# Attention with decay and a SwiGLU FFN in one kernel: K and Q transposed by DMA, decay moved into V

## Chip, cores, metric

The kernel runs on one core of a Trainium2 chip. The metric is device time in microseconds (us) of one launch. The profile is one execution taken by the hardware profiler. TensorE is PE in it (PEld its weight loads), VectorE DVE, ScalarE ACT, GpSimd POOL, SyncE SP.

## The reference

Eight batches, eight heads, 576 tokens, 64 elements per head; then an FFN over 4608 tokens of width 512, inner width 1536.

```python
scores = scale * np.matmul(q, k.transpose(0, 1, 3, 2))
cum = np.cumsum(np.maximum(s, 0.0), axis=-1)
bias = -(cum[:, :, :, None] - cum[:, :, None, :])
scores = np.where(causal, -1000000000.0, scores + np.minimum(bias, 0.0))
attn = softmax(scores)                    # max subtracted, sum + 1e-9
x = np.matmul(attn, v)                    # heads side by side: 4608 x 512
xn = x / np.sqrt(np.mean(x * x, -1) + 1e-6) * rms_g
g = xn @ w_gate
out = (g * sigmoid(g) * (xn @ w_val)) @ w_out
```

The part of the bias that depends on the query cancels in the softmax. What is left is a factor exp(cum) of the key.

## The kernel before

**Two streams of work.** The FFN runs in 9 chunks of 512 tokens (`ffn`). A chunk has 12 blocks of 128 inner columns, each with four gate matmuls (line 632, "G") and four value matmuls (641, "V"), and then four output blocks of 12 matmuls (654, "O"). ACT makes a tanh of the gate (635); DVE makes U (644) and Ht (637) of it.

Attention is cut into small steps that are put between the FFN's groups. After each group the program calls `step`, one slot: 36 slots in a chunk. `step` looks at queues written by hand (`s_seq`, `av_seq`, `xt_seq`, `t_seq` and the side queues) and issues what is ready, by lags counted in slots (`can_s`, `can_av`, `can_t`). All this is settled when the program is built. On the chip each engine goes through its own list in order and waits on semaphores.

**One attention batch.** A batch has five token blocks (four of 128, one of 64).

- K and Q come from memory as float32 on the SP queue (batches 0 and 1) or the ACT queue, four tokens (1 KB) in a piece (`load_kq`), the last 64 tokens apart (`load_kq_tail`). POOL, ACT or DVE cast them to bf16 (`cast`, `cast_x`, lines 138, 140, 148).
- For batches 0 and 1, and for K throughout, TensorE transposes (`t_step`, 173; `tail_step`, 189) and ACT or DVE copies out of PSUM. Q of later batches is transposed by a DMA on SP (`kq_dma`, 160).
- `s_step` (236): the scores of one key block against its own and the next query block, for four heads: four matmuls of 256 columns into one double bank of PSUM (`psS`, one buffer). One exponential per head follows on ACT (260), because its bias is a column per head: `biasK` holds the cumulated decay, less half of its range. POOL masks the diagonal block (269).
- `av_step` (286, 292): values for one query block and four heads; the 65th column of V is 1, so that it yields the sum. DVE divides (299, 301).
- The norm: sum of squares on ACT (307), two small operations on POOL (314, 317), scaling on DVE (324), a transposing DMA to `xnT` on SP (334), or TensorE in batch 0 (343).

V is loaded and cast by POOL's DMA queue (`load_v`, 164), as are the FFN weights (`load_w`, two halves each, 666). A range check of K and Q runs on DVE (`check_mag` 355, `check_max` 361). If it fails, a second, slow path (`general`) computes all again; it does not run with these inputs.

**The start.** The first four token blocks of batch 0 are done before the FFN's first chunk, in an order written out by hand, with some filling matmuls (`warm`).

Of the kernel before, what the change touches and what calls it, by code (L numbers as in the profile page):

```python
# [26 lines left out]
def kernel(  # L27
# [22 lines left out]
    HP = H // 2  # L50
    NV = 65
# [19 lines left out]
    pp = fast.enter_context(tc.tile_pool(name="pp", bufs=1, space=bass.MemoryType.PSUM))  # L71


    xnT = mp.tile([128, CC, RING], BF16, name="xnT")

    kq32 = mp.tile([128, 2, H, 320], FP32, name="kq32")
    kqn = mp.tile([128, 2, 2, NSC, H, D], BF16, name="kqn")
    kqT = mp.tile([128, 2, 2, HP * 640], BF16, name="kqT")


    kqTn = kqT.rearrange("d a w (h n) -> d a w h n", h=HP)
    kqTx = kqT.rearrange("d a w (c h n) -> d a w c h n", c=NSC, h=HP)
    XB = 2
    v_sb = mp.tile([128, 2, NSC, H, NV], BF16, name="v_sb")

# [5 lines left out]
    biasK = mp.tile([128, NSC, BH], FP32, name="biasK")  # L91
# [3 lines left out]
    mag = mp.tile([128, H * 320], BF16, name="mag")  # L95
# [3 lines left out]

    def psF():  # L100
        return pp.tile([128, DM], FP32, name="psF", tag="F", bufs=4)

    def psF16():
        return pp.tile([128, 8, 128], BF16, name="psF16", tag="F", bufs=4)

    def psS():
        return pp.tile([128, 2, 512], FP32, name="psS", tag="S", bufs=1)

    def psAV():
        return pp.tile([128, 512], FP32, name="psAV", tag="AV", bufs=1)  # L110

    def psAV16():
        return pp.tile([128, 8, 128], BF16, name="psAV16", tag="AV", bufs=1)

    def psT():
        return pp.tile([128, 8, 128], BF16, name="psT", tag="T", bufs=1)

    def psT32():
        return pp.tile([128, 512], FP32, name="psT32", tag="T", bufs=1)


    def load_kq(eng, b, w, h0=0, h1=H):
        src = k if w == 0 else q
        eng.dma_start(
            out=kq32[:, w, h0:h1, 0:256],
            in_=src[b, h0:h1, 0:512, :].rearrange("h (p r) d -> p h (r d)", r=4))

    def load_kq_tail(eng, b, w):
        src = k if w == 0 else q
        eng.dma_start(  # L130
            out=kq32[0:64, w, :, 256:320],
            in_=src[b, :, 512:576, :].rearrange("h p d -> p h d"))

    def cast(eng, b, w, r0, r1, h0=0, h1=H):
        o = kqn[:, b % 2, w, r0:r1, h0:h1, :]
        i = kq32[:, w].rearrange("p h (r d) -> p r h d", d=D)[:, r0:r1, h0:h1, :]
        if eng is nc.scalar:
            eng.activation(out=o, in_=i, func=AF.Copy)  # L138
        else:
            eng.tensor_copy(out=o, in_=i)  # L140

    def cast_x(eng, b, w, hp):

        if hp < HP:
            o = kqn[:, b % 2, w, 0:4].rearrange("p r h d -> p (r h d)")[:, hp * 512:hp * 512 + 512]
            o = o.rearrange("p (r h d) -> p h r d", r=4, h=2)
            i = kq32[:, w, 2 * hp:2 * hp + 2, 0:256].rearrange("p h (r d) -> p h r d", d=D)
            eng.tensor_copy(out=o, in_=i)
        else:
            cast(eng, b, w, 4, 5)  # L150

    def kq_dma(b, w, c):

        if c < 4:
            src = kqn[32 * c:32 * c + 32, b % 2, w, 0:4].rearrange("p r h d -> p (r h d)")
            dst = kqTx[:, b % 2, w, c].rearrange("d h (r p) -> d (h r) p", r=4)
        else:
            src = kqn[0:64, b % 2, w, 4].rearrange("p h d -> p (h d)")
            dst = kqTx[:, b % 2, w, 4, :, 0:64]
        nc.sync.dma_start_transpose(out=dst, in_=src)  # L160

    def load_v(b, c):
        n = rows(c)
        nc.gpsimd.dma_start(  # L164
            out=v_sb[0:n, b % 2, c, :, 0:64],
            in_=v[b, :, c * 128:c * 128 + n, :].rearrange("h p d -> p h d"))


    def t_step(b, hp, w, pT=None, dve=None):
        pT = psT() if pT is None else pT  # L170
        dve = (w == 1) if dve is None else dve
        for r in range(4):
            nc.tensor.matmul(  # L173
                pT[:, r, :], lhsT=kqn[:, b % 2, w, r, 2 * hp:2 * hp + 2, :],
                rhs=ident_bf, is_transpose=True, start=(r == 0), stop=(r == 3))
        dst = kqTn[:, b % 2, w, hp, 0:512].rearrange("d (p r) -> d p r", r=4)
        src = pT[:, 0:4, :].rearrange("d r p -> d p r")
        if dve:
            nc.vector.tensor_copy(out=dst, in_=src)
        else:  # L180
            nc.scalar.activation(out=dst, in_=src, func=AF.Copy)

    def tail_step(b):
        pT = psT()
        nw = 2 if b < XB else 1
        for w in range(nw):
            for hp in range(HP):
# [5 lines left out]
        if b == 0:  # L193
            nc.vector.tensor_copy(out=dst, in_=src)
        else:
            nc.scalar.activation(out=dst, in_=src, func=AF.Copy)
# [14 lines left out]
    def slot_free():  # L211
        return eread.get(ecount[0] % NE, 0) == 0
# [850 lines left out]
```

## Time and profile before

| | |
|---|---|
| median of 3 runs | 384.63 us (384.48 to 384.88) |
| profiled execution, first to last instruction | 383.2 us |
| granted TensorE clock, mean | 0.995 |
| TensorE busy | 349.6 us (91%) |
| VectorE, ScalarE, GpSimd busy | 286.1, 247.4, 172.7 us |
| exponentials (line 260) | 352, 114.3 us busy |
| first FFN matmul | at 32.36 us |
| DMA | 46.24 MB, 103292 packets, of them 78481 under 512 B |

The time around the span is not in the profile; the runs are 1.3 to 1.7 us above it. Busy times of engines overlap. Matmuls are pipelined, so the distance between the starts of two groups tells more than the duration in a row.

### The profile page before, as it was taken

Reading aid. Unit: us, or ns where it says so; the run is one execution under the profiler, and the core shown is the slowest. Engines: PE = TensorE matmul, PEld = TensorE weight load, DVE = VectorE, ACT = ScalarE, POOL = GpSimd, SP = SyncE. Lnnn points to the kernel's source line nnn. Section 1 sums busy time; section 2 is a strip of 40 time slices with the busy share of each in tenths; the row PEclk is TensorE's granted clock in tenths of the full one; section 3 lists DMA queues with packets and bytes.
Section 4 is the critical chain, followed back from the end, with each engine's and each line's share of the span. In section 5 each row is a group of like instructions: output and inputs, shape, how many; then the busy total and the mean of one; then the engine's idle time right before and its main releaser. Section 6 shows DMA issues by size and latency. Waiting matters only on the chain. (4 is left out here: it accounts for less than half of the span.)

```text
span 383.2 us, 7015 instructions
## 1 busy us (share of the span) xinstructions
PE 349.6 (91%) x2391; PEld 165.5 (43%) x2436; DVE 286.1 (75%) x525; ACT 247.4 (65%) x646; POOL 172.7 (45%) x277
## 2 busy tenths in 40 slices
PE   1767999899999999999989999999999999999992
PEld 1443544444444444444434444444444444444441
DVE  6768988499888879987988977984388539837720
ACT  3777787457886687768678757776986774323311
POOL 5866725956774496619734764362223220000000
PEclk9999999999999999999999999999999999999997
DMA  7999999999998896796559083981200221020011
GB/s 232 183 229 232 141 221 179 149 200 196 131 187 214 172 173 98 197 201 51 78 186 225 16 89 92 122 63 42 98 15 9 55 98 21 3 83 28 2 56 60
DMA packets 103292, 46.24 MB, mean 121 GB/s; under 512 B 78481, under 2 KB 98449, under 8 KB 103249
## 3 DMA queue, kind: packets, MB, share of 16 engines
q0 software_dynamic: 41168, 9.44, 30.5%
q1 hardware_dynamic: 43184, 21.97, 26.6%
q10 hardware_dynamic: 18896, 14.30, 15.3%
q8 instruction: 21, 0.34, 0.4%
q14 instruction: 23, 0.18, 0.2%
HBM read 38.16 MB, written 9.44 MB: 124 GB/s over the span
## 5 line engine op out<-in xcount | busy, mean ns | idle before, releaser
L260 ACT ACTIVATE E<-psS,biasK 128x256 bf16<-128x256 f32 (+3 forms) x352 | 114.3, 427 | 8.7 <-PE psS L236 7.6
L641 PE MATMUL psF<-xnT,wv_sb 128*128 128x512 bf16 x417 | 110.0, 380 | 1.0 <-DVE Ht L637 0.2
L632 PE MATMUL psF<-xnT,wg_sb 128*128 128x512 bf16 x419 | 109.1, 379 | 1.8 <-ACT xnT L350 0.7
L654 PE MATMUL psF<-wout_sb,Ht 128*128 128x512 bf16 x416 | 100.8, 379 | 0.8 <-issue 0.2
L269 POOL TENSOR_SCALAR_AFFINE_SELECT E<-E 128x512 bf16<-128x512 bf16 x72 | 52.8, 733 | 94.8 <-ACT E L260 94.1
L635 ACT ACTIVATE T<-psF 128x512 f32<-128x512 f32 x108 | 64.5, 600 | 46.8 <-PE psF L632 40.1
L644 DVE SCALAR_TENSOR_TENSOR U<-T,psF 128x512 bf16<-128x512 f32 x108 | 73.7, 682 | 22.3 <-ACT T L635 22.1
L637 DVE TENSOR_TENSOR Ht<-U,psF 128x512 bf16<-128x512 bf16 x99 | 67.6, 683 | 7.1 <-PE psS L236 0.5
L632 PEld LDWEIGHTS <-wg_sb 128*128 128x128 bf16 x432 | 38.9, 97 | 42.8 <-issue 4.8
L654 PEld LDWEIGHTS <-Ht 128*128 128x128 bf16 x432 | 38.6, 98 | 42.8 <-issue 3.3
L641 PEld LDWEIGHTS <-wv_sb 128*128 128x128 bf16 x432 | 38.1, 98 | 43.0 <-issue 6.4
L324 DVE SCALAR_TENSOR_TENSOR xs_sb<-x_sb,al_all,g_row 128x512 bf16<-128x512 bf16 (+1 forms) x40 | 33.6, 842 | 16.0 <-POOL al_all L317 15.2
L307 ACT ACTIVATE xs_sb<-x_sb 128x512 bf16<-128x512 bf16 (+1 forms) x36 | 22.8, 637 | 32.5 <-DVE x_sb L301 31.8
L659 ACT ACTIVATE osb<-psF 128x512 f32<-128x512 f32 x36 | 21.7, 602 | 28.2 <-PE psF L654 20.2
L164 POOL DMA_DIRECT2D v_sb<-in_v_dram x40 | 35.4, 884 | 0.0
L140 POOL CAST kqn<-kq 128x512 bf16<-128x512 f32 (+1 forms) x46 | 32.6, 728 | 3.9 <-DMA kq<-in_k_dram 3.9
L361 DVE TENSOR_TENSOR acc<-acc,mag 128x1280 bf16<-128x1280 bf16 x32 | 32.4, 1034 | 0.3
L314 POOL TENSOR_SCALAR al_all<-ss_all 128x1 f32<-128x1 f32 (+1 forms) x40 | 10.9, 272 | 45.2 <-ACT xs_sb L307 40.2
L236 PE MATMUL psS<-kqT 64*128 64x256 bf16 (+2 forms) x304 | 26.6, 261 | 3.7 <-ACT E L260 2.5
L292 PEld LDWEIGHTS <-E 128*128 128x128 bf16 x320 | 22.3, 99 | 13.9 <-POOL E L269 3.5
L173 PE MATMUL psT<-ident_bf,kqn 128*128 128x128 bf16 x124 | 13.9, 227 | 12.2 <-ACT kqn L138 8.3
L317 POOL TENSOR_TENSOR al_all<-al_all,mhalf 128x1 f32<-128x1 f32 (+1 forms) x40 | 23.2, 581 | 3.3
(93 smaller groups left out, 288.3 us busy)
## 6 DMA issues: line engine op xcount, KB each, us to landing
out_dram<-osb SPq DMA_DIRECT2D x36, 256.0 KB, 2.2
kq<-in_q_dram ACTq DMA_DIRECT2D x6, 1024.0 KB, 8.5
kq<-in_k_dram ACTq DMA_DIRECT2D x6, 1024.0 KB, 7.7
v_sb<-in_v_dram POOLq DMA_DIRECT2D x32, 128.0 KB, 4.6
wg_sb<-in_moe_w_gate_dram POOLq DMA_DIRECT2D x2, 768.0 KB, 7.3
wv_sb<-in_moe_w_val_dram POOLq DMA_DIRECT2D x2, 768.0 KB, 10.4
wout_sb<-in_moe_w_out_dram POOLq DMA_DIRECT2D x1, 1536.0 KB, 14.4
kq<-in_k_dram SPq DMA_DIRECT2D x2, 512.0 KB, 6.5
```

The lines of the kernel that those rows point to most:

```text
L140: eng.tensor_copy(out=o, in_=i)
L164: nc.gpsimd.dma_start(out=v_sb[0:n, b % 2, c, :, 0:64], in_=v[b, :, c * 128:c * 128 + n, :].rearrange("h p d -> p h d"))
L260: nc.scalar.activation(out=eo, in_=ei, func=AF.Exp, scale=0.125, bias=biasK[:, kb, bh:bh + 1])
L269: nc.gpsimd.affine_select(out=Ev[:, :, 0:nq], in_=Ev[:, :, 0:nq], pattern=[[0, nh], [1, nq]], compare_op=ALU.is_ge, fill=0.0, base=0, chan ...
L324: nc.vector.scalar_tensor_tensor(out=xs_sb[0:n, (b * NSC + qb) % NX, :], in0=x_sb[0:n, (b * NSC + qb) % NX, :], scalar=al_all[0:n, col:col ...
L361: nc.vector.tensor_tensor(out=acc[:, sl], in0=acc[:, sl], in1=mag[:, sl], op=ALU.max)
L632: nc.tensor.matmul(Gp, lhsT=wg_sb[:, cc, fs], rhs=xnT[:, cc, x0:x0 + DM], start=(cc == 0), stop=(cc == CC - 1))
L635: nc.scalar.activation(out=T, in_=Gp, func=AF.Tanh, scale=0.5)
L637: nc.vector.tensor_tensor(out=Ht[:, fb - 1, :], in0=pend[0], in1=pend[1], op=ALU.mult)
L641: nc.tensor.matmul(Vp, lhsT=wv_sb[:, cc, fs], rhs=xnT[:, cc, x0:x0 + DM], start=(cc == 0), stop=(cc == CC - 1))
L644: nc.vector.scalar_tensor_tensor(out=U, in0=T, scalar=1.0, in1=Gp, op0=ALU.add, op1=ALU.mult)
L654: nc.tensor.matmul(Op, lhsT=Ht[:, fb, tb * 128:(tb + 1) * 128], rhs=wout_sb[:, fb, :], start=(fb == 0), stop=(fb == FB - 1))
```

## The change

- K and Q are loaded by token blocks, one block of one tensor for all heads at a time, cast by the DMA on POOL's queue (pieces of 64 float32). One transposing DMA on SP turns a block of K and Q together. TensorE transposes only in batch 0.
- Decay: `wK` = exp(cum less half of its range) for each key and head is made once. V is loaded as float32 on SP and multiplied by `wK` (`weigh_v`: POOL, in batch 0 DVE). The column of ones becomes `wK` itself (`weigh_one`).
- With no bias left, an exponential covers four heads. `s_step` issues the matmuls of all eight heads in one run, into two buffers of a PSUM tile `psW`, which `av_step` shares. `av_step` does eight heads in one tile, with one reciprocal and one division.
- The sum of squares is always on ACT (`x_sum`). The range check reads the transposed K and Q.
- Weights come in thirds. Values may follow scores after 4 slots (before 5). The hand-written order of the start is new, and the lags are others; attention steps end in chunk 5 of the built order (before: chunk 7).

The core of the diff:

```diff
+    def load_kq(b, c, w):
+        n = rows(c)
+        nc.gpsimd.dma_start(
+            out=kq[0:n, b % 2, c, w].rearrange("p (h d) -> p h d", d=D),
+            in_=(k if w == 0 else q)[b, :, c * 128:c * 128 + n, :].rearrange("h p d -> p h d"))
+
+    def kq_dma(b, c):
+        n = rows(c)
+        nc.sync.dma_start_transpose(
+            out=kqT[:, b % 2, c].rearrange("d w h n -> d (w h) n")[:, :, 0:n],
+            in_=kq[0:n, b % 2, c].rearrange("p w e -> p (w e)"))
...
+        nc.sync.dma_start(
+            out=v32[0:n, b % 2, c],
...
+    def weigh_v(eng, b, c):
+        n = rows(c)
+        eng.tensor_tensor(
+            out=v_sb[0:n, b % 2, c, :, 0:D], in0=v32[0:n, b % 2, c],
+            in1=wK[0:n, c, b * H:(b + 1) * H].unsqueeze(2).to_broadcast([n, H, D]), op=ALU.mult)
+
+    def weigh_one(eng, b):
+        eng.tensor_copy(out=v_sb[:, b % 2, :, :, D], in_=wK[:, :, b * H:(b + 1) * H])
...
-                    nc.scalar.activation(out=eo, in_=ei, func=AF.Exp, scale=0.125,
-                                         bias=biasK[:, kb, bh:bh + 1])
...
+        for g in ((0,) if kb == 4 else (0, 1)):
+            e = take_slot((b, kb, g), 1 if kb == 4 else 2)
+            ps = psW()
+            hps = range(HP) if kb == 4 else (2 * g, 2 * g + 1)
+            for j, hp in enumerate(hps):
+                for par in (0, 1):
...
+                    nc.tensor.matmul(
+                        ps[:, par, j * W:(j + 1) * W], lhsT=kqT[rs, p, kb, 0, hp, :], rhs=qT,
+                        start=(j == 0), stop=(j == len(hps) - 1))
...
+            def exps(eo=eo, ei=ei):
+                nc.scalar.activation(out=eo, in_=ei, func=AF.Exp, scale=0.125)
...
+            if c == NSC - 1:
+                check(b)
+            if b + 2 < B:
+                t = slot[0]
+                loads(b + 2, lambda: slot[0] >= t + 6 and slot[0] % 2 and phase() < 30)
...
+        return ready(4, "S", b, qb) and (b == 0 or ready(3, "V", b, qb))
...
-        fs = slice(i * (DF // 2), (i + 1) * (DF // 2))
+        fs = slice(i * (DF // 3), (i + 1) * (DF // 3))
...
+    def decay_exp(ps):
+        nc.scalar.activation(out=wK.rearrange("p a e -> p (a e)"), in_=ps[:, 0:NSC * BH], func=AF.Exp)
...
+        load_kq(0, 0, 0)
+        load_kq(0, 0, 1)
+        make_identity(nc, ident_bf)
+        load_kq(0, 1, 1)
+        load_kq(0, 1, 0)
...
+        t_step(0, 0, True)
+        t_step(0, 1, True)
+        t_step(1, 1, True)
+        s0 = scores(0)
+        s0[0][0]()
+        s0[1][0]()
+        ps = decay_turn()
...
+        check(0)
+        loads(1, lambda: True)
+        dma_side.insert(6, (lambda: True, lambda: load_w(moe_w_gate, wg_sb, 2)))
+        dma_side.insert(7, (lambda: True, lambda: load_w(moe_w_val, wv_sb, 2)))
+        dma_side.append((lambda: True, lambda: nc.gpsimd.dma_start(
+            out=wout_sb, in_=moe_w_out.rearrange("(fc p) d -> p fc d", p=128))))
+        values(1, lambda: slot[0] >= 8)
+        weighs(1)
```

In `step`, a slot now takes from the SP queue either a transposing DMA or a V load, and from POOL's two queues (`dma_side`, `pool_side`) one entry; a mask of the step before goes ahead of them.

## The prediction

> **What bounds the kernel now.** I read the page's busy times first, then the windows, then TensorE's timeline.
>
> ```profile
> span 383.2 us, 7015 instructions
> PE 349.6 (91%) x2391; PEld 165.5 (43%) x2436; DVE 286.1 (75%) x525; ACT 247.4 (65%) x646; POOL 172.7 (45%) x277
> ```
>
> A matmul's end is modelled, so 91% alone proves little. The windows (PE, PEld, DVE, ACT, POOL busy in each stretch) say more:
>
> ```profile
> 184.00:222.00 38.00, 36.23 (x272) 16.90 (x276) 32.99 (x60) 30.73 (x85) 21.29 (x34) 1.00 0.61 127
> 345.00:376.50 31.50, 31.18 (x142) 14.03 (x145) 17.51 (x31) 9.32 (x18) 0.00 (x0) 1.00 0.09 35
> ```
>
> The second row is a chunk of FFN alone: 31.2 us for 144 matmuls, 0.216 us each. The first is about a chunk with attention mixed in: it lasts some 39 us. So TensorE's order sets the time, and attention costs what it puts into that order. TensorE's timeline prices each piece by the distance of starts:
>
> ```profile
> 45.12 1.03 PE L632 MATMUL psF<-xnT,wg_sb 128*128 128x512 bf16 x4
> 46.08 0.39 PE L236 MATMUL psS<-kqT 64*128 64x256 bf16 x4
> 46.41 0.40 PE L173 MATMUL psT<-ident_bf,kqn 128*128 128x128 bf16 x4
> 46.64 1.03 PE L641 MATMUL psF<-xnT,wv_sb 128*128 128x512 bf16 x4
> 47.50 0.39 PE L173 MATMUL psF<-ident_bf,kqn 128*128 128x128 bf16 x4
> ```
>
> Four FFN matmuls take 0.86 us (46.64 to 47.50), but 0.96 ahead of scores (45.12 to 46.08): entering scores costs 0.10. Four score matmuls take 0.33 less rounding, 0.32; a transposing step of four 0.22, 0.055 each. Values are 0.0305 each (eight in 0.24 to 0.25 elsewhere in this timeline); eight 64-column scores take 0.22 plus the 0.10.
>
> The sum for before, from the first FFN matmul at 32.36 to the last one's end near 376.4: FFN 1296 x 0.216 = 279.9; scores 56 x 0.42 + 8 x 0.32 = 26.1; values 520 x 0.0305 = 15.9; K and Q transposes (128 + 36) x 0.055 = 9.0; x transposes 8 x 0.055 = 0.4. Total 331.3. The stretch is 344.0, so 12.7 us are stalls: on single-buffered score PSUM, on K copies in chunk 0, on the last x tile of chunk 0 (1.5 us). Around it lie 32.4 us of start and 383.2 - 376.4 = 6.8 us of end. The runs' median, 384.63, is 1.4 us above this span; I add that at the end.
>
> **Part 1, transposes leave TensorE.** The built order of the changed kernel has no K or Q transpose after the start: -9.0 us on the path. Batches 1 to 7 need 35 transposing DMAs instead, twice the size of today's 30.
>
> **Part 2, eight score matmuls in one run.** 28 runs replace 56 steps of 256 columns: 28 x (0.64 + 0.10) = 20.7 against 23.5, -2.8 us. The built order does show eight in a row, so that rival is out. Values keep their 520 matmuls.
>
> So TensorE's own work is 279.9 + 20.7 + 2.6 + 15.9 + 0.4 = 319.5 us.
>
> **Part 3, one exponential per four heads.** These are the rows (line, engine, operation, shapes, count, busy us, mean ns):
>
> ```profile
> L260 ACT ACTIVATE E<-psS,biasK 128x256 bf16<-128x256 f32 x180 | 71.9, 484 | 4.5 <-PE psS L236 3.4 <-DVE biasK L684 0.5 <-issue 0.2
> L659 ACT ACTIVATE osb<-psF 128x512 f32<-128x512 f32 x36 | 21.7, 602 | 28.2 <-PE psF L654 20.2 <-remote 5.0 <-PEq L892 2.0
> L140 POOL CAST kqn<-kq 128x512 bf16<-128x512 f32 x42 | 29.8, 727 | 0.1
> L164 POOL DMA_DIRECT2D v_sb<-in_v_dram x40 | 35.4, 884 | 0.0
> L269 POOL TENSOR_SCALAR_AFFINE_SELECT E<-E 128x512 bf16<-128x512 bf16 x72 | 52.8, 733 | 94.8 <-ACT E L260 94.1
> ```
>
> ACT took 415 ns for 256 elements (the first casts) and 602 for 512, 0.73 ns per element; 1024 come to 0.97 us. 64 of these and 8 of 0.6 make 67 us against 114.3 on ACT. The K copies (some 23 us) go as well. ACT was not the bound, so this shortens only the chain from scores to values.
>
> That chain gets less room. Values now come 4 slots after their scores, formerly 5. By the built order, score run, four FFN groups, values: 0.75 + 4 x 0.866 = 4.2 us from the first score to the first value, 4.45 to the second half. In between: 0.45 to the first half's scores, 0.97 exponential, a tanh (0.6) that must await its FFN group and so ends at 2.2, the second exponential to 3.2, its mask on POOL 0.73: 3.95. The margin is 0.5 us, when nothing is ahead of the mask on POOL. I put 0.15 us of wait on each of 36 value steps, 5 us (bounds 0 and one POOL issue of 0.88 each).
>
> **Part 4, POOL.** Per batch it now has 10 K/Q loads x 0.88, five weighings, one copy of the ones column (0.3), 9 masks x 0.73 and 5 pairs for the norm at 0.85: the weighing has no row. It reads two tensors where the cast reads one: between 0.73 and twice that; I take 1.1, midway. 8.8 + 5.0 + 0.3 + 6.6 + 4.3 = 25.0 us, with bounds 23.3 and 26.6, in the 33.8 us that TensorE gives a batch ((319.5 + 11 - 3 x 31.2) / 7: attention now ends in chunk 5, and three chunks are FFN alone). So POOL is 74% full, with masks queued behind loads. The Trainium skill (GPSIMD Engine Reference, section 3.1) puts a two-input elementwise operation on that engine at about 2.6 cycles per element at 1.2 GHz, by which 512 elements would be an estimated 1.1 us. No run here shows it; it would leave POOL at 25.0.
>
> **Part 5, DMA.** K and Q come in pieces of 256 B (today 1 KB), through POOL's queue like V today; V moves to SP. Three windows of 1 us in which the DMA engines were full (at 41, 206 and 201 us) price packets:
>
> ```profile
> q0 software_dynamic: 1207, 0.16, 240.6%
> q10 hardware_dynamic: 364, 0.37, 105.2%
> q1 hardware_dynamic: 916, 0.26, 129.8%
> ```
>
> The first is V alone, 1207 pieces of 256 B read, 0.31 MB per us; the second K/Q alone in 1 KB, 0.37 MB; the third mostly transposes. Per batch: 13.5 blocks x 1024 / 1207 = 11.5 us, K/Q transposes 4608 / 916 = 5.0, x 2.8, output about 2.5: 22 us of 33.8. It hides, outside chunk 0. There the last third of the gate weights is issued some 7 us after the FFN starts and needed at 15, and the output weights are issued at 15 and needed near 26; today they took 14.4 us to land. 2 us of stall (0 to 5). SP's in-order queue gets 35 transposes at 1.24 us today, perhaps 2.5 at double size, 12 us per batch, ahead of x transposes and stores: with five x transposes at 1.2 and the loads about 22 of 33.8, hidden by the half batch or more between load and use.
>
> The Trainium skill (DMA: Bandwidth & Descriptors, Specifications) speaks against this part: line rate needs at least 512 B, and below it the engine does a read-modify-write. The rows differ: 256 B gave 0.31 MB per us against 0.37 with 1 KB. By the rule the loads could take twice as long, which is the second rival.
>
> **Part 6, start.** Today:
>
> ```profile
> 26.67 0.64 POOL L269 TENSOR_SCALAR_AFFINE_SELECT E<-E 128x512 bf16<-128x512 bf16 x1
> 31.72 0.60 ACT L350 ACTIVATE xnT<-psF 128x512 bf16<-128x512 bf16 x1 [0.88 <-PE psF L343]
> 32.36 1.02 PE L632 MATMUL psF<-xnT,wg_sb 128*128 128x512 bf16 x4 [0.69 <-ACT xnT L350]
> ```
>
> The last mask ends at 27.3, the FFN starts 5 us later. New: the first loads are issued from 0.9 us at 0.9 each and land 3.4 to 4.8 later, the third (Q block 1) near 7.3; transposes and copy, scores at 8.6, exponentials 9.2 to 11.2. The next pairs, with block 2's and 3's copies between on ACT, 12.9 to 14.8 and 16 to 18, then a sum of squares, the last 19.6 to 21.5. POOL's masks stand behind the norm pairs: the last ends near 25. Then values, x, sum, norm, scale, transpose, copy as today, 5 us: FFN at 29.5, range 27 to 32.5. No cast is left, and that is the gain, 2.9 us.
>
> **Sum.** 29.5 + 319.5 + 11 of stalls (5 values, 2 weights, 4 of today's that the change leaves, such as those on DVE) + 6.8 = 366.8, + 1.4 = 368.2 us. VectorE does a little less per batch (one 512-wide division at 0.68 for two of 0.42): 14.9 us with scaling 4.2, reciprocals 1.0 and the range check 6.3. With 24 FFN operations of 0.68 and 7/6 batches a chunk needs 33.8 us of it in 39.4: close, not the bound.
>
> **Rivals.**
> First, masks come late: POOL's in-order queue has a load issue or a weighing ahead of the second mask, and values wait for it. For: 74% full, a 0.5 us margin, operations that reached 1.2 us today. Against: it waited 94 us for ACT in total, and it is not saturated. Each 0.1 us on 36 steps is 3.6 us; over 0.15 + 16.4 / 36 = 0.6 us each, the kernel is slower. With 0.88 each: 394 us. Chance 0.10.
> Second, DMA becomes the bound. V alone, unqueued, showed 32 ns per packet and engine (44% of 38 us for 8460), 2.0 us per block. At that price loads take 27.5 us per batch, transposes (4608 + 2560 packets) 14.3, output 2.5: 44 us, 10 over 33.8, times 7 batches: 438 us. It decides above 36 us per batch. Against: 1207 in one us when queued. Chance 0.05.
> Third, the start gains nothing, because ten loads are issued one by one and TensorE starts the FFN at half rate (four score matmuls spanned 0.61 us at 13.3 and 0.39 at 46): FFN at 36, 375 us. Chance 0.08.
> Fourth, stalls nearly vanish (5 us) and the start takes 27: 360 us. Chance 0.07. The forecast keeps 0.70.
>
> Range: 360 to 386, from the fourth case to the lower half of the first. A measurement of this kernel tells about 0.2% from no change. Faster: 0.70 + 0.08 + 0.07 less 0.02 that falls within 0.2% = 0.83; slower 0.15.
>
> **What would show it.** Right: no K/Q transpose on TensorE after the start; eight scores within 0.75 us; first FFN matmul near 29.5; three last chunks of 31.2; DMA slices not full between 80 and 250 us. Wrong: TensorE idle on E from POOL by more than 10 us, idle on kqT from a DMA, or weights late in chunk 0 by more than 5.

## The result: 12% slower, and the profile after

The changed kernel took 430.97 us (median of four runs; 426.69 to 432.74) against 384.65 for the kernel before on the same chip: a ratio of 1.119, 95% interval 1.113 to 1.124. The forecast was 368.2, faster. It was wrong in its sign and outside its range.

The profiled execution took 432.74 us, span 431.1. Page of the changed kernel:

```profile
span 431.1 us, 6360 instructions
...
PE 354.8 (82%) x2270; PEld 165.1 (38%) x2270; DVE 285.6 (66%) x431; ACT 181.8 (42%) x314; POOL 202.3 (47%) x289
...
PEclk9968956698979989995999999999999999999997
DMA  9999999969999999994998999330022001011011
...
DMA packets 172824, 46.21 MB, mean 107 GB/s; under 512 B 163376, under 2 KB 167984, under 8 KB 172784
```

TensorE's share fell from 91% to 82% although it has less to do. The DMA row stands at 9 in nearly every slice of the first two thirds of the span. The bytes are those of before (46.24 MB), the packets 172824 instead of 103292.

The windows from one chunk's first gate matmul to the next (chunks 0 to 6; PE, PEld, DVE, ACT, POOL busy, PEclk, DMA share, GB/s):

```profile
36.75:102.33 65.58, 46.51 (x289) 20.83 (x289) 36.80 (x54) 21.12 (x36) 32.91 (x45) 0.79 1.29 145
102.33:154.75 52.42, 40.54 (x265) 18.28 (x264) 36.64 (x49) 22.03 (x38) 36.97 (x51) 0.90 1.27 165
154.75:204.13 49.38, 41.98 (x289) 18.72 (x288) 42.49 (x53) 24.00 (x41) 37.90 (x48) 0.89 1.25 138
204.13:247.04 42.91, 38.19 (x286) 18.01 (x283) 34.80 (x50) 22.43 (x40) 32.70 (x44) 1.00 1.22 142
...
288.58:327.61 39.03, 37.57 (x286) 17.76 (x283) 27.82 (x46) 20.83 (x39) 11.36 (x22) 1.00 0.17 48
327.61:359.02 31.41, 31.23 (x150) 14.10 (x147) 17.73 (x28) 9.92 (x18) 0.72 (x2) 1.00 0.10 36
```

This is where the time went. Chunk 5, where transfers have ended, and chunk 6, FFN alone, are what was forecast. Chunk 0 takes 65.6, chunks 1 and 2 52.4 and 49.4, chunk 3 still 42.9. By the forecast's own terms (319.5 of work and 11 of stalls) a chunk with attention has (330.5 - 3 x 31.2) / 6 = 39.5, so chunks 0 to 5 (290.9 in all) lost 54 us, the start 7.2 (FFN at 36.75, forecast 29.5), and chunks 6 to 8 with the end 3.

Who made TensorE wait, in the list of waits:

```profile
PE psW L184 <- DMA kqT<-kq: 20.1, 4, 10.2
...
PEld L221 <- POOL E L200: 13.4, 18, 1.4
...
PE psW L221 <- POOL E L200: 9.4, 10, 1.3
...
PE psW L184 <- DVE x_sb L234: 8.9, 8, 4.9
PE psF L273 <- DVE xs_sb L255: 8.0, 4, 3.9
```

Scores waited four times, up to 10.2 us, for transposed K and Q (`kqT`) from a DMA (PEld, the weight load ahead of a matmul, meets the same waits and is not added). Values waited for masks on POOL (`E`, the exponentials that it masks). Scores waited for VectorE to empty the tile `psW`. Summed over TensorE's timeline, the waits in chunks 0 to 5 come to 48 us, and FFN groups slower than 0.864 us add 12. The slow groups stand behind the waits:

```profile
77.44 1.03 PE L184 MATMUL psW<-kqT 64*128 64x256 bf16 x8 [10.19 <-DMA kqT<-kq]
78.41 1.89 PE L502 MATMUL psF<-xnT,wg_sb 128*128 128x512 bf16 x4
80.09 1.91 PE L511 MATMUL psF<-xnT,wv_sb 128*128 128x512 bf16 x4
```

After 10 us idle, groups start 1.7 us apart instead of 0.86; the granted clock was 0.50 from 77.4 to 82.5 us, and the clock row shows 5 and 6 in such slices.

### The profile page after: what moved, and what is told of

It reads as the page before. It is cut to its first block, busy times and chain, and to the rows that moved or that the text cites. A ratio compares the mean times of both kernels' runs of the same rounds, so it can differ in the third digit from the quotient of the medians.

```text
span 431.1 us, 6360 instructions
## 1 busy us (share of the span) xinstructions
PE 354.8 (82%) x2270; PEld 165.1 (38%) x2270; DVE 285.6 (66%) x431; ACT 181.8 (42%) x314; POOL 202.3 (47%) x289
## 2 busy tenths in 40 slices
DMA packets 172824, 46.21 MB, mean 107 GB/s; under 512 B 163376, under 2 KB 167984, under 8 KB 172784
## 5 line engine op out<-in xcount | busy, mean ns | idle before, releaser
L502 PE MATMUL psF<-xnT,wg_sb 128*128 128x512 bf16 x432 | 114.2, 388 | 3.8 <-DVE U L514 2.3
L511 PE MATMUL psF<-xnT,wv_sb 128*128 128x512 bf16 x432 | 114.4, 388 | 3.1 <-DMA wv_sb<-in_moe_w_val_dram 3.1
L197 ACT ACTIVATE E<-psW 128x1024 bf16<-128x1024 f32 (+1 forms) x72 | 68.6, 969 | 22.7 <-PE psW L184 22.3
L200 POOL TENSOR_SCALAR_AFFINE_SELECT E<-E 128x512 bf16<-128x512 bf16 x72 | 51.7, 720 | 37.4 <-ACT E L197 36.7
L511 PEld LDWEIGHTS <-wv_sb 128*128 128x128 bf16 x432 | 41.7, 99 | 53.9 <-issue 4.2
L502 PEld LDWEIGHTS <-wg_sb 128*128 128x128 bf16 x432 | 40.6, 100 | 53.4 <-issue 11.6
L524 PEld LDWEIGHTS <-Ht 128*128 128x128 bf16 x432 | 41.3, 100 | 50.0 <-issue 7.5
L255 DVE SCALAR_TENSOR_TENSOR xs_sb<-x_sb,al_all,g_row 128x512 bf16<-128x512 bf16 (+1 forms) x40 | 49.9, 1248 | 13.7 <-POOL al_all L248 9.4
L184 PE MATMUL psW<-kqT 64*128 64x256 bf16 (+1 forms) x320 | 26.9, 284 | 31.8 <-DMA kqT<-kq 20.1
L127 POOL TENSOR_TENSOR v_sb<-v,wK 128x512 bf16<-128x512 f32 (+1 forms) x35 | 40.9, 1171 | 0.9 <-DMA v<-in_v_dram 0.7
L529 ACT ACTIVATE osb<-psF 128x512 f32<-128x512 f32 x36 | 21.3, 593 | 40.2 <-PE psF L524 32.8
L109 POOL DMA_DIRECT2D kq<-in_k_dram x40 | 35.5, 889 | 1.1 <-POOLq L904 0.8
L109 POOL DMA_DIRECT2D kq<-in_q_dram x40 | 35.5, 889 | 0.0
L221 PE MATMUL psW<-v_sb,E 128*128 128x65 bf16 x320 | 27.0, 200 | 9.7 <-POOL E L200 9.4
L184 PEld LDWEIGHTS <-kqT 64*128 64x128 bf16 x320 | 11.7, 100 | 52.5 <-issue 19.8
L291 DVE TENSOR_TENSOR acc<-acc,mag 128x1280 bf16<-128x1280 bf16 x32 | 31.2, 991 | 0.4
## 6 DMA issues: line engine op xcount, KB each, us to landing
wv_sb<-in_moe_w_val_dram POOLq DMA_DIRECT2D x3, 512.0 KB, 10.6
wout_sb<-in_moe_w_out_dram POOLq DMA_DIRECT2D x1, 1536.0 KB, 26.3
```

The costliest lines, as they stand in the source:

```text
L109: nc.gpsimd.dma_start(out=kq[0:n, b % 2, c, w].rearrange("p (h d) -> p h d", d=D), in_=(k if w == 0 else q)[b, :, c * 128:c * 128 + n, :]. ...
L127: eng.tensor_tensor(out=v_sb[0:n, b % 2, c, :, 0:D], in0=v32[0:n, b % 2, c], in1=wK[0:n, c, b * H:(b + 1) * H].unsqueeze(2).to_broadcast([ ...
L184: nc.tensor.matmul(ps[:, par, j * W:(j + 1) * W], lhsT=kqT[rs, p, kb, 0, hp, :], rhs=qT, start=(j == 0), stop=(j == len(hps) - 1))
L197: nc.scalar.activation(out=eo, in_=ei, func=AF.Exp, scale=0.125)
L200: nc.gpsimd.affine_select(out=Ev[:, :, 0:nq], in_=Ev[:, :, 0:nq], pattern=[[0, nh], [1, nq]], compare_op=ALU.is_ge, fill=0.0, base=0, chan ...
L255: nc.vector.scalar_tensor_tensor(out=xs_sb[0:n, col % NX, :], in0=x_sb[0:n, col % NX, :], scalar=al_all[0:n, col:col + 1], in1=g_row[0:n], ...
```

## Experiments

All times are from one execution each, beside a run of the kernel before at 384.2 to 385.0. "FFN" is the start of the first gate matmul; c0 to c5 are the chunks' lengths, from TensorE's timeline. Rows of 2 KB mix up heads and tokens, and kernels without late weights or without weighing leave work out; the others do all the work.

| kernel | us | FFN | c0 | c1 | c2 | c3 | c4 | c5 |
|---|---|---|---|---|---|---|---|---|
| before | 384.9 | 32.4 | 44.3 | 39.2 | 39.6 | 38.7 | 40.2 | 39.3 |
| changed | 432.7 | 36.8 | 65.6 | 52.4 | 49.4 | 42.9 | 41.5 | 39.0 |
| changed, again | 428.0 | 35.2 | 61.0 | 53.4 | 49.4 | 42.9 | 41.5 | 39.0 |
| rows of 2 KB | 411.9 | 33.6 | 56.0 | 46.9 | 48.1 | 42.8 | 40.3 | 39.0 |
| no late weights | 412.8 | 36.9 | 45.9 | 50.8 | 50.2 | 43.3 | 41.6 | 39.0 |
| no weighing | 409.9 | 35.0 | 57.1 | 51.1 | 42.9 | 39.7 | 40.3 | 39.1 |
| these three | 390.2 | 37.1 | 43.3 | 44.0 | 43.0 | 39.8 | 39.6 | 39.0 |
| V later in the start | 440.0 | 45.3 | 61.5 | 52.9 | 49.4 | 45.9 | 41.5 | 39.0 |
| weighing on VectorE | 427.5 | 39.5 | 60.6 | 53.6 | 44.2 | 43.2 | 42.8 | 39.0 |
| weights earlier | 427.4 | 38.9 | 53.9 | 53.3 | 49.4 | 46.0 | 41.5 | 39.0 |
| K, Q through SP | 417.3 | 35.9 | 56.7 | 49.4 | 43.2 | 51.1 | 40.5 | 37.4 |
| distances | 417.9 | 38.7 | 58.1 | 41.3 | 49.8 | 43.5 | 43.0 | 37.5 |
| the three, and distances | 390.8 | 36.8 | 53.8 | 37.0 | 40.8 | 39.4 | 40.3 | 37.5 |
| several repairs | 420.2 | 39.1 | 62.2 | 40.7 | 46.9 | 45.0 | 43.8 | 37.5 |
| second thirds later | 428.6 | 34.6 | 63.7 | 52.4 | 49.4 | 42.9 | 41.6 | 39.0 |
| A: early batch 1, distances | 416.1 | 38.3 | 51.8 | 45.9 | 49.6 | 47.1 | 40.4 | 37.4 |
| A, V of batches 2 to 4 on VectorE | 417.6 | 39.1 | 51.7 | 48.6 | 49.1 | 45.8 | 40.3 | 37.4 |
| A, V on VectorE | 412.1 | 35.8 | 53.2 | 49.0 | 45.1 | 44.4 | 41.3 | 38.0 |
| B: A with rows of 2 KB | 398.2 | 33.0 | 47.0 | 42.2 | 47.4 | 46.5 | 39.3 | 37.4 |
| B without weighing | 379.5 | 33.1 | 45.3 | 40.0 | 39.6 | 40.0 | 38.2 | 38.0 |

The theories: A, the number of pieces of 256 B; B, the order of the transfer queues (later: and the planned distances); C, POOL's weighing, its queue and what it does to VectorE. The letters in the quoted expectations mean these, not the kernels A and B of the table.

**The same kernel again.**

> The changed kernel once more, unaltered, for the spread of its stages. The start and chunk 0 hold transfers that meet in a different order in each run (start 35.0 to 39.5 us in kernels whose start is the same): expected is a start within 3 us of 36.75, chunk 0 between 57 and 66, chunks 2 to 5 within 1 us of 49.4, 42.9, 41.5 and 39.0.

Chunks 1 to 5 came back within 1 us, start and chunk 0 moved by 1.6 and 4.6. Chunk 3 took 46 in two kernels (V later, weights earlier) that differ only ahead of it. So I count a difference from 2 us in chunks 1, 2, 4 and 5, above 3 in chunk 3, and from 5 in start and chunk 0. Whole runs of the changed kernel spread over 6 us (426.7 to 432.7), so a smaller difference between two runs decides nothing by itself.

**Three cuts, one by one.**

Rows of 2 KB (V alike), no late weights, no weighing:

```diff
-            in_=(k if w == 0 else q)[b, :, c * 128:c * 128 + n, :].rearrange("h p d -> p h d"))
+            in_=(k if w == 0 else q).rearrange("b h s d -> b (h s d)").rearrange(
+                "b (p e) -> b p e", e=HD)[b, c * 128:c * 128 + n, :])
...
-        dma_side.insert(6, (lambda: True, lambda: load_w(moe_w_gate, wg_sb, 2)))
-        dma_side.insert(7, (lambda: True, lambda: load_w(moe_w_val, wv_sb, 2)))
-        dma_side.append((lambda: True, lambda: nc.gpsimd.dma_start(
-            out=wout_sb, in_=moe_w_out.rearrange("(fc p) d -> p fc d", p=128))))
...
-            weigh_v(nc.gpsimd, b, c)
+            if b < 2:
+                weigh_v(nc.gpsimd, b, c)
```

> This kernel reads each block of K, Q and V as rows of 2 KB that lie together in memory, the same bytes and the same number of transfers, but an eighth of the pieces on the reading side (so heads and tokens are mixed up in what is computed). Theory A, the transfer engines are slowed by the number of 256-byte pieces: the waits of TensorE on kqT from a DMA (38 us in the changed kernel) nearly vanish, chunk 0 shortens from 65.6 to about 45, chunks 1 and 2 from 52 and 49 to about 40, and the run takes 390 us or less. Theory B, K and Q stand in POOL's queue of transfers behind the weights and bytes, not pieces, set the pace: 5 to 15 us less, with the waits on kqT in chunk 0 still there. Theory C, POOL and VectorE hold each other up: chunks 1 to 4 stay within 3 us of the changed kernel's, the run above 415.

The run took 411.9, between the theories and nearest to B. Chunk 0 keeps waits on kqT (8.6 us), chunk 1 is 5.5 to 6.5 shorter. Pieces cost, but they are not all. Packets fell to 76056. The long rows also relieve POOL: issuing a load of K or Q took it 0.59 us instead of 0.89, some 24 us less over 80 loads, so this run does not tell the transfers from POOL's time.

> This kernel does not load the last thirds of the gate and value weights and the output weights; a constant stands in for them. Theory B, K and Q of batches 1 and 2 stand behind these transfers in POOL's queue: the three waits on kqT at 61, 77 and 121 us go, chunk 0 shortens by 15 to 20 us to about 47 and chunk 1 by 5, the run takes about 405. Theory A, the pieces of 256 bytes alone saturate the engines: chunk 0 shortens by 5 to 8 us (the bytes of the weights), chunks 1 and 2 by under 3, the run takes about 422. Theory C, POOL and VectorE: chunk 0 alone changes, by under 5.

The run took 412.8, not 405. Chunk 0 falls to 45.9 with no wait on kqT left in it; chunks 1 and 2 stay. So most of chunk 0's loss is that of the late weights, and they cost the other chunks little. The changed kernel's timeline (start, us, engine) shows how:

```profile
50.38 1.05 POOL L720 DMA_DIRECT2D wout_sb<-in_moe_w_out_dram  x1
...
61.59 7.97 SPq L115 DMA_TRANSPOSE kqT<-kq  x2
69.61 9.82 SPq L121 DMA_DIRECT2D v<-in_v_dram  x4
```

And the page's list of DMAs (KB written, median us from issue to landing):

```profile
wout_sb<-in_moe_w_out_dram POOLq DMA_DIRECT2D x1, 1536.0 KB, 26.3
```

The output weights, issued at 50.38 on POOL's queue, land 26.3 us later. The transposing DMAs go out on SP meanwhile: two take 8 us to issue, and scores get their data at 77.4. The longest landing of a kqT transfer was 15.8 us here, 7.0 without the late weights.

The loads ahead of those transposing DMAs were late as well. K and Q of batch 1's last blocks stand behind the last thirds of the gate and value weights, which POOL issued at 43.9 and 44.7 (the same columns, for DMAs issued from 44 to 51 us; block 3):

```profile
kq<-in_k_dram POOLq DMA_DIRECT2D x1, 128.0 KB, 14.1
kq<-in_q_dram POOLq DMA_DIRECT2D x1, 128.0 KB, 13.5
```

They took 13.5 to 14.1 us to land, against 4.8 to 5.3 for the same blocks without the late weights. Q landed at 61.5, and SP, which had waited for it for 4.9 us, issued the transposing DMA at 61.59.

That transfers of several queues share an engine's time is what the Trainium skill states (DMA: Bandwidth & Descriptors, Queues, rings and completion order): an engine takes packets in turn from each queue that has work. The landing times agree.

> This kernel leaves out POOL's weighing of V for batches 2 to 7 (values of batches 0 and 1 are used again); loads and all else stay. Theory C, POOL's longer queue and its shared access with VectorE: the scaling on VectorE (1.25 us on average) returns toward 0.75, TensorE's waits on E from POOL (23 us) go under 8, chunks 2 to 4 shorten by 15 us together, the run takes about 410. Theories A and B (transfers): the waits on E shorten too, but chunks 0 to 2 keep their lengths within 3 us each, and the run stays above 422.

The run took 409.9: chunks 2 to 4 shorten by 6.5, 3.2 and 1.2, 11 us together where 15 were expected. Waits on E fall from 9.4 to 4.5. (Start and chunk 0 gained too, within what a repeat moves.) In the changed kernel one scaling on VectorE took 5.79 us while POOL ran without a pause (its timeline, other engines left out):

```profile
187.08 5.79 DVE L255 SCALAR_TENSOR_TENSOR xs_sb<-x_sb,al_all,g_row 64x512 bf16<-64x512 bf16 x1 [0.73 <-POOL al_all L248]
187.16 0.94 POOL L109 DMA_DIRECT2D kq<-in_k_dram  x1
...
188.12 0.65 POOL L200 TENSOR_SCALAR_AFFINE_SELECT E<-E 128x512 bf16<-128x512 bf16 x1
188.72 1.05 POOL L127 TENSOR_TENSOR v_sb<-v,wK 128x512 bf16<-128x512 f32 x1
...
189.72 0.63 POOL L200 TENSOR_SCALAR_AFFINE_SELECT E<-E 128x512 bf16<-128x512 bf16 x1
190.30 0.94 POOL L109 DMA_DIRECT2D kq<-in_q_dram  x1
...
191.26 3.24 POOL L127 TENSOR_TENSOR v_sb<-v,wK 128x512 bf16<-128x512 f32 x2
```

The next `x_sb` came late, and scores waited 4.9 us for their tile, until 196.8. Undisturbed, the scaling takes 0.74. The Trainium skill (SBUF — State Buffer, Who interferes with whom) says that a VectorE instruction with two inputs in SBUF contends with a GpSimd instruction that reads SBUF. The trace agrees in that the scaling was long beside such instructions; here it lasted through a whole row of them, and which of the row held it up is not shown. Between 90 and 290 us the longest scaling was 1.49 us without the weighing and 1.21 with it on VectorE. How much of the 11 us is this and how much the masks behind POOL's weighing, no run tells apart.

**The three together.**

> This kernel joins the three cuts tried one by one: K, Q and V in rows of 2 KB, no late weights, no weighing on POOL for batches 2 to 7 (values, heads and weights are not those of the reference). If pieces, queue order and POOL's weighing are the causes, and nothing else of size, the waits of TensorE in chunks 0 to 4 fall from 47 us to under 10, chunks 0 to 4 take 38 to 41 each, and the run takes 368 to 376. If something else costs time too (clock, transposing DMAs, planned distances that are too short), waits on kqT stay above 5 us and the run is above 382.

The run took 390.2, above the 382 that meant "something else too". Some 3.8 us of it are the constants that VectorE writes in the start in place of the weights, for which TensorE waits. Chunk 1 still waits 5.3 us on kqT, and chunks 1 and 2 take 43 to 44.

**Distances in the plan.**

```diff
-        return ready(7, "L", b, c) and ...
+        return ready(10, "L", b, c) and ...
-        return b == 0 or all(ready(5, "X", b, c) ...)
+        return b == 0 or all(ready(8, "X", b, c) ...)
```

> This kernel only plans larger distances: a block's transposing DMA 10 slots behind its loads instead of 7, and scores 8 slots behind the transposing DMAs instead of 5 (a slot is one group of four FFN matmuls, 0.86 us). Distance theory: in chunk 1 load to scores takes 12.6 us where 12 slots give 10.5, so TensorE meets the waits on kqT there only because the plan is too short; with 18 slots the waits on kqT in chunks 1 and 2 (9 to 11 us) go below 3, chunk 1 takes 44 to 47, and the run is 5 to 10 us shorter (less some 2 us for three more slots spent ahead of chunk 1). Rival, throughput: what is loaded late stays late, the wait moves to the end of the chunk or to the values, and the run stays within 3 us of 431.

The run took 417.9, 10 to 15 less; no wait on kqT is left, chunk 1 takes 41.3. The distances were too short. Chunk 0 now waits 5.0 us on the output weights and 4.2 on the scaling instead, so the order of the transfers still costs it. My pairing in the expectation was wrong for chunk 1, though: the late part there is the transposing DMA alone. It was issued at 113.11 and landed 7.7 us later, behind four loads of V on the same queue; the scores were planned 5 slots, 4.3 us, behind (timeline of the changed kernel):

```profile
108.32 4.63 SPq L121 DMA_DIRECT2D v<-in_v_dram  x4
...
113.11 3.49 SPq L115 DMA_TRANSPOSE kqT<-kq  x1
...
120.83 1.03 PE L184 MATMUL psW<-kqT 64*128 64x256 bf16 x8 [5.66 <-DMA kqT<-kq]
```

> The kernel with wide rows, without late weights and without POOL's weighing for batches 2 to 7, with the larger planned distances as well (outputs as in that kernel). If distances are the rest of the loss on kqT, the 5.3 us of waits on kqT in chunk 1 go and the run takes 383 to 387; what then is left over the forecast is the start (37) and TensorE's waits on x_sb and xs_sb from VectorE (some 10 us). If it stays at 389 or more, distances aren't it.

The run took 390.8, a miss. Chunk 1 fell to 37, but chunk 0 grew by 10.5. The later plan pushed batch 1's chain against the start of chunk 1, which needs its x.

**Other ways to relieve the queues.**

V later in the start:

```diff
-        touch(0)
-        touch(1)
-        nc.sync.dma_start(out=g_row, ...)
         decay_sums()
...
         t_step(1, 0, False)
+        touch(0)
+        touch(1)
...
         touch(3)
+        nc.sync.dma_start(out=g_row, ...)
```

> This kernel issues the V loads of batch 0's first two blocks and the load of the norm's weights later in the start, behind the first K and Q blocks; nothing else moves. If these transfers are what held up the third K/Q load (6.1 us from issue to landing), the first scores come near 9 us instead of 11.7 and the first FFN matmul near 33.5 instead of 36.75, and the run is about 3 us shorter. If the 256-byte pieces or POOL's one-by-one issue set the start, the first scores stay within 1 us of 11.7 and the FFN within 1 us of 36.75.

The opposite: scores came at 9.7 instead of 11.7, as hoped, but V itself was then late (a wait of 6.4 us on `v_sb`), and the FFN began at 45.3.

Weights earlier:

```diff
         s3[1][0]()
+        load_w(moe_w_gate, wg_sb, 2)
+        load_w(moe_w_val, wv_sb, 2)
...
-        dma_side.insert(6, (lambda: True, lambda: load_w(moe_w_gate, wg_sb, 2)))
-        dma_side.insert(7, (lambda: True, lambda: load_w(moe_w_val, wv_sb, 2)))
```

> This kernel issues the last thirds of the gate and value weights during the start (ahead of the last masks, when the transfer engines are half idle) instead of behind the first three blocks of batch 1; the output weights stay. Queue theory: K and Q of batch 1's blocks 3 and 4 no longer stand behind them, the waits on kqT in chunk 0 fall from 10.8 us to under 4 and those on weights (3.8) go, chunk 0 takes 50 to 54 instead of 57 to 66. Rival, the bytes cost the same wherever they are issued: the start grows by 4 to 8 us and the sum of start and chunk 0 stays within 3 us of the changed kernel's (92 to 102).

Chunk 0 took 53.9 and the waits on weights went. One wait on kqT of 6.8 stayed: a transposing DMA took 10.3 us to issue at 54, while the output weights moved. Start and chunk 0 came to 92.8, against 96 to 102, but chunk 3 took 3 us more and the run, 427.4, is not shorter.

Weighing on VectorE:

```diff
-            weigh_v(nc.gpsimd, b, c)
+            weigh_v(nc.vector, b, c)
```

> This kernel weighs V on VectorE instead of POOL in all batches, the same operations in the same places; nothing else changes and nothing is left out. POOL theory (its queue and its shared access with VectorE): TensorE's waits on E from POOL go under 8 us, the longest scaling on VectorE falls from 5.8 us to about 1.2, chunks 2 to 4 shorten by 10 us together, run 412 to 420. Rival, VectorE becomes the bound: it takes 40 operations of 0.84 more, 34 us, and TensorE's waits on VectorE (x_sb, U) grow by as much as those on E shrink, run 426 or more.

The time came out on the rival's side, though its mechanism is not shown: TensorE's waits on x_sb did not grow (8.9 to 7.0). Waits on E shrank (9.4 to 7.2) and the longest scaling was 1.2, as the POOL theory said, but only chunk 2 gained (5.2). Chunks 3 and 4 took 0.3 and 1.3 more, which does not count by the repeat, and the run is a repeat's distance from the changed kernel.

K and Q through SP, cast on ScalarE (the last thirds in the start as above, three blocks of batch 1 loaded in the start too, and one buffer for the cast blocks instead of two):

```diff
+    kq32 = mp.tile([128, 3, 2, HD], FP32, name="kq32")
...
+        nc.sync.dma_start(
+            out=kq32[0:n, (b * NSC + c) % 3, w].rearrange("p (h d) -> p h d", d=D),
+            in_=(k if w == 0 else q)[b, :, c * 128:c * 128 + n, :].rearrange("h p d -> p h d"))
...
+        nc.scalar.activation(out=kq[0:n, 0, c], in_=kq32[0:n, (b * NSC + c) % 3], func=AF.Copy)
```

> In this kernel K and Q of batches 1 to 7 are loaded as 4-byte values by SP's queue, 256-byte pieces as before, and ScalarE casts each block (1024 elements, an estimated 1 us, from the 1.02 us of the exponential of that size); the late weight thirds are issued in the start. POOL no longer issues 70 loads of 0.89 us, and nothing of K and Q stands behind weights. If POOL's time and queue are the main cause, waits on E and on kqT both fall by half or more and the run takes 390 to 405. If the 256-byte pieces are, the same number of them still has to pass, the waits on kqT stay above 15 us, and the run takes 415 or more.

The run took 417.3, and neither side came out. Waits on kqT halved (10.3), those on E did not (12.4), although POOL was busy 35%: mask and weighing still share a queue. The casts waited 20 us for data on ScalarE, ahead of tanh.

Several repairs (with the weighing on VectorE, and 9 and 7 slots):

```diff
         do_av((0, 3))
+        load_w(moe_w_gate, wg_sb, 2)
+        load_w(moe_w_val, wv_sb, 2)
...
+        for i, at_ in enumerate((4, 7, 10)):
+            dma_side.insert(at_, (lambda: True, lambda i=i: load_out(i)))
```

> A whole kernel that does all the work of the reference: V weighed on VectorE, the last thirds of gate and value weights issued at the end of the start, the output weights in three pieces between K and Q of batch 1, distances of 9 and 7 slots. If queue order, distances and POOL's queue are the larger causes, chunk 0 takes 46 to 52, chunk 1 45 to 48, and the run 403 to 412. If the number of 256-byte pieces sets the pace in chunks 0 and 1, which this kernel does not change, it takes 418 or more. Either way it is not expected below the kernel before.

The run took 420.2, where the expectation had put the theory of pieces, but the trace shows a cause beside the pieces. Chunk 1 fell to 40.7, chunk 0 stayed at 62.2: kqT waits of 13.4 us, since pieces of the output weights now stood ahead of batch 1's later blocks (17.2 us to land, 512 KB each). A queue's order was made worse by the repair.

**What sets start and chunk 0.**

Second thirds later:

```diff
-        load_w(moe_w_gate, wg_sb, 1)
-        load_w(moe_w_val, wv_sb, 1)
...
         do_av((0, 3))
+        load_w(moe_w_gate, wg_sb, 1)
+        load_w(moe_w_val, wv_sb, 1)
```

> This kernel issues the second thirds of the gate and value weights about 13 us later in the start, behind the last norm pair instead of ahead of the values of block 0. If they are what holds up the loads of V blocks 2 to 4 (SP took 12.6 us to issue four of them, from 14.3 us on), the wait of TensorE on the last norm scalings (2.7 to 5.9 us) goes below 1.5 and the first FFN matmul comes at 31 to 33.5 instead of 35 to 39; chunk 0 then waits for these weights by 0 to 5 us. If the start is set by K and Q pieces and single issues alone, the FFN still starts at 34.5 or later.

TensorE's wait on the first scaling went from 2.7 (in the repeat) to 1.1, yet the FFN started at 34.6, within a repeat's spread. These weights do not set the start. The 12.6 us of the expectation were misread, too: SP issued two loads of V at 14.29 and 14.70, in 0.4 and 0.6 us, and then waited 10.2 us for a write of VectorE into their tile before it issued the other two.

A: batch 1's first three blocks in the start (with 10 and 8 slots):

```diff
         load_w(moe_w_val, wv_sb, 1)
+        load_kq(1, 0, 0)
+        load_kq(1, 0, 1)
...
         s3[1][0]()
+        load_kq(1, 1, 0)
+        load_kq(1, 1, 1)
...
         do_av((0, 3))
+        load_kq(1, 2, 0)
+        load_kq(1, 2, 1)
...
-        dma_side.insert(6, (lambda: True, lambda: load_w(moe_w_gate, wg_sb, 2)))
-        dma_side.insert(7, (lambda: True, lambda: load_w(moe_w_val, wv_sb, 2)))
+        dma_side.insert(0, (lambda: True, lambda: load_w(moe_w_gate, wg_sb, 2)))
+        dma_side.insert(1, (lambda: True, lambda: load_w(moe_w_val, wv_sb, 2)))
```

> This kernel has the distances of 10 and 8 slots, loads K and Q of batch 1's first three blocks during the start, and then the last weight thirds ahead of its blocks 3 and 4. Theory, chunk 0 is as long as batch 1's chain from its first load to its last x tile, and that chain starts too late and stands behind weights: chunk 0 takes 46 to 51 instead of 58 to 66, chunk 1 about 41, the run 400 to 408. Rival, the transfers of the start and chunk 0 together are the limit (20 MB up to the start of chunk 1): the start grows by 3 to 6 us, start and chunk 0 together stay at 94 to 97 as with the distances alone, the run 413 or more.

Neither side came out. Start and chunk 0 took 90.1, less than either kind of repair alone, but the run stayed at 416.1, and chunks 1 to 3 lost what start and chunk 0 gained over the distances alone. Order and distances move the loss about.

```diff
-            weigh_v(nc.gpsimd, b, c)
+            weigh_v(nc.vector if b in (2, 3, 4) else nc.gpsimd, b, c)
```

> As the kernel with the early K and Q of batch 1, and V of batches 2, 3 and 4 weighed on VectorE, those of other batches on POOL. If POOL's weighing is what lengthens chunk 2 (49.4) through VectorE's scaling of 5.8 us and late masks, chunk 2 takes 44 and the run is 4 to 6 us below the kernel with the early K and Q; chunks 3 and 4 stay within 1 us. If VectorE has no room in chunk 2 either, the two stay within 2 us.

There is no gain (417.6), but the run does not answer the question: VectorE had weighed batch 4 by 157 us, and POOL weighed batch 5 at 177 to 187, inside chunk 2 (139 to 188), beside a scaling of 6.8 us. Hence one more, A with all weighings on VectorE:

```diff
-            weigh_v(nc.gpsimd, b, c)
+            weigh_v(nc.vector, b, c)
```

> A whole kernel: early K and Q of batch 1, distances of 10 and 8, and V of every batch weighed on VectorE. In the run with batches 2 to 4 on VectorE, POOL weighed batch 5 at 177 to 187 us, inside chunk 2, beside a scaling of 6.8 us, so that run did not tell whether VectorE has room. If POOL's weighing is what lengthens chunk 2 and VectorE has room for it, no scaling takes over 1.5 us between 90 and 290, chunks 2 and 3 take 43 to 45 (49.6 and 47.1 with POOL), and the run 408 to 412. If VectorE has no room, waits on x_sb and U grow instead, chunks 2 to 4 together stay within 2 us of 137, and the run at 414 or more.

The run took 412.1: chunks 2 and 3 took 45.1 and 44.4, the longest scaling 1.48. VectorE has room for part of it: chunks 2 to 4 are 6.3 us shorter than in A, against 15 between B and B without weighing.

B is A with the rows of 2 KB (the first diff); the next leaves the weighing out as well.

> The kernel with the early K and Q of batch 1 and the larger distances, now with K, Q and V read in rows of 2 KB (same bytes; heads and tokens mixed up). If the 256-byte pieces are what keeps start and chunk 0 at 90 us and gives chunk 1 its waits on kqT back, start and chunk 0 together come to 78 to 83, the waits on kqT go below 3, chunk 1 takes 41, and the run 398 to 404. If the bytes, or the order of batch 1's chain, are the limit, start and chunk 0 stay at 87 or more and the run at 409 or more.

The run took 398.2, as the theory of pieces said: start and chunk 0 at 80.0, chunk 1 at 42.2. One wait on kqT of 5.6 in chunk 0 stayed, where less than 3 was expected. The window from 40 to 90 us of A (columns as above):

```profile
40.00:90.00 50.00, 40.97 (x279) 19.42 (x284) 36.70 (x53) 21.30 (x37) 29.27 (x39) 0.88 1.33 171
```

and the same of B:

```profile
40.00:90.00 50.00, 39.60 (x271) 18.43 (x275) 38.16 (x55) 20.97 (x37) 31.46 (x46) 0.90 0.89 172
```

The GB/s are the same, but the DMA share is 1.33 against 0.89: packets overlap in this share, so it can exceed 1, and it falls by a third where the pieces are long. POOL gained as well, as above: its loads took 23 us less to issue, and TensorE's waits on E fell from 11.4 to 5.3 us, those on kqT from 9.7 to 5.6. So the 18 us from A to B are the gain of long rows in both ways, and their shares are not shown.

> As the one with early K and Q of batch 1, larger distances and rows of 2 KB, and without POOL's weighing of V for batches 2 to 7. If the weighing (POOL's queue, VectorE's scaling) is the rest, chunks 2 to 4 take 40 to 41 each where they took 47 to 50, 43 to 47 and 40 to 43, and the run comes to 384 to 390. If chunks 2 and 3 stay above 43 even so, what lengthens them is something else, such as the two shared score and value tiles in PSUM that VectorE must empty.

The run took 379.5, better than expected: chunks 2 and 3 at 39.6 and 40.0. That speaks against the shared PSUM tiles as the rest of the loss: scores still waited for VectorE to empty them, but only 3.8 us in all. Waits that are left in it (lines are numbered two higher there):

```profile
PE psW L186 <- DMA kqT<-kq: 6.3, 2, 4.0
...
PE psW L186 <- DVE x_sb L236: 3.8, 7, 0.9
...
PE psW L223 <- POOL E L202: 1.6, 6, 0.5
```

This is the one kernel below the kernel before, and it leaves work out. Among kernels that do all the work none came near 384.65; A with V on VectorE, at 412.1, was the best, so the runs point to no whole version that beats both.

So the loss, as a ladder of single runs from the repeat: 428.0, less 11.9 for order and distances, less 18.0 for long rows, less 18.6 without weighing, is 379.5. The first step would be 10.6 to 16.6 from other runs of the changed kernel, and the sizes hold for this order of the steps. Taken singly the changes give 10 to 18 us each, and the first three together 38 where their sum is 50: they share waits. What is left over the forecast, 11 us, is the start (33.1 against 29.5) and the rest of the waits.

## Why the prediction was wrong, by its steps

The sum allowed 11 us of stalls; TensorE waited 48 us in chunks 0 to 5, 20 of them on kqT, for which the sum had nothing.

- **TensorE's own work (parts 1 and 2): right.** No K or Q transpose after the start; chunk 6 took 31.4 us (31.2 forecast); the changed kernel's chunks 0 to 5, less waits and slow groups, are 290.9 - 60 = 231 us where 319.5 - 3 x 31.2 = 226 was forecast.
- **Part 3: sizes right, margin wrong.** The exponential of 1024 took 1.02 us (0.97). The margin of 0.5 us did not hold: values waited 9.4 us on masks, 10 times up to 1.3, against 5 us planned on 36 steps. That is the first rival's mechanism, at under a third of its price of 0.88 us on each of 36 steps.
- **Part 4: the price was right, the cover was missing.** The weighing took 1.17 us (1.1), also for the block of 64 tokens, which the sum of 25.0 had counted as half; POOL was 71 to 77% busy in chunks 1 to 3 (74). I costed it at nothing because POOL had room. Without it chunks 2 to 4 were 11 us shorter in the changed kernel and 15 in B. It cost that in two ways: masks behind it, for which part 3 held 5 us, and VectorE's scaling, for which the sum had nothing, 0.84 us before, 1.25 on average and up to 5.8 after. "Close, not the bound" left VectorE no room to lose that.
- **Part 5 failed, and it is the largest miss.** In the ladder order, distances and long rows come to 30 us, the weighing of part 4 to 18.6. Each is more than the 16.4 us by which the forecast lay below the kernel before, so each alone could turn the sign: B, without most of part 5's loss, is still slower at 398.2. "22 us of 33.8 per batch, it hides" is a sum of throughput, taken from windows in which one kind of transfer ran. What decided were landing times under several queues against distances in the plan. "Hidden by the half batch or more between load and use" was not read from the plan: the transposing DMA has 5 slots, 4.3 us, and took 4.2 at the median, 7.7 at 113 us and 15.8 at 61.6. "2 us of stall for weights" were 3.8 on the weights themselves and 10.8 on what shared the engines with them; chunk 0 without them was 15 to 20 us shorter.
- **The second rival** stood for one of the causes, pieces of 256 B, at a chance of 0.05 and with a wrong form: not a steady 44 us per batch (chunks 4 and 5 are nearly free of it) but a start and three chunks in which weights and two batches share the engines. The rule of the Trainium skill that spoke against this part (DMA: Bandwidth & Descriptors, Specifications: at least 512 B for line rate) was set aside on rows of 0.31 and 0.37 MB per us. Rows of 2 KB took 16 to 18 us off, part of them through POOL's shorter issues; the rule's side was the better guide, though no run shows a read-modify-write, and "twice as long" was my estimate, not the page's.
- **Part 6: 7 us off.** The third load landed at 10.4 instead of 7.3, scores came at 11.7 instead of 8.6, TensorE waited 4.5 us on scalings at its end, VectorE 3.7 on loads of V. The third rival had named the start (36). Long rows gave 33.0 to 33.6; the order of V and weights gave nothing. Without the loads of V and of the norm's weights ahead, the first scores came at 9.7, and V was late instead. What else keeps the start from 29.5 was not tried apart.
- **Its signs were the right ones**: it named TensorE idle on E, on kqT, and late weights as what would show it wrong. The wait on kqT, 20.1 us, is clear; the one on E is at its mark of 10 (9.4, in the repeat 10.6), the one on weights, 3.8, below its mark of 5. Of the signs for it, DMA slices not full between 80 and 250 us did not come: the row stands at 9 there.

## What to carry to other kernels

A transfer is hidden when it lands before it is used, not when its engines have time left. Take the landing time under load from the trace, the distance between issue and use from the built order, and look at what stands ahead in the same queue and beside it in others. And an engine that is three quarters busy is not free: ask who shares its queue and its way to memory.

## What the runs showed of the chip that was not expected

- A transposing DMA on SP, usually 1.2 to 1.3 us to issue, took up to 10.3 while 1536 KB of weights moved on POOL's queue, and four loads of V behind such transfers took 9.8 us to issue at 69.61, two of them some 4 us each where 0.6 is usual. SP issued the next transfer only after that.
- One VectorE instruction of 0.74 us took 5.8 beside back-to-back work on POOL, 6.8 in A. In B without weighing the longest still took 2.5.
- Larger distances moved 10 us of loss into chunk 0 without shortening the run when the three cuts were already made (390.8 against 390.2).
